# The second layer's first matmul in Strassen's seven products, in blocks of 1024 tokens

## The chip, the cores and the metric

One core of one Trainium2 chip runs the whole program. The metric is device microseconds (us) of one execution, the median of several runs.

## The reference

Chunked attention with eight memory keys per head (4 x 8 heads, 768 positions, 64 wide) gives 3072 tokens of 512. Two layers follow, each with `w_in` (512 x 2048) and `w_out` (2048 x 512):

```python
h = x @ w_in;  g = h - np.tanh(h);                              x = g @ w_out   # first layer
h = x @ w_in;  g = np.maximum(h, 0) + alpha * np.minimum(h, 0); y = g @ w_out   # second layer
```

The weights arrive as 64-bit floats. `alpha` is a vector of 2048.

## The kernel before

Tokens lie in 24 tiles of 128. Each layer takes them in six blocks of four tiles (512 columns); `d_ff` is cut into 16 slices `f` of 128. Every float is split into a high and a low part of the matmul's own 32-bit type, and a product of two floats is three passes (`PASS`: high-high, high-low, low-high). So `emit_h` (L166) issues 12 matmuls for one slice (4 depths of 128 by 3 passes) and `emit_y` (L201) issues 12 more into four PSUM banks that gather `y` over the 16 slices; the h of the next slice is issued ahead of the y of this one. Between them stands `emit_g` (L181): in the second layer two VectorE (DVE) instructions (L191, L194), then the split of g, high part on ScalarE (ACT, L197), low part on GpSimd (POOL, L198). `evac_y` (L223) copies the banks to SBUF and stores them: `y1d` in DRAM after layer one, the output after layer two.

Attention (`emit_scores`, `emit_soft`, `emit_pv`) makes the operand tiles of layer one in the double ring `ring`, four tiles ahead of time at the start and then one every 20 us or so by a plan. In one tile of it POOL multiplies the exponentials `sc` by the reciprocal of their sum (L332), DVE transposes them into `et` (L336), ACT and DVE copy `et` into `ebuf`, PE multiplies by v, and ACT and DVE split the result into `ring` (L361, L362).

Weights: `load_raw` brings 64-bit words, `to_f32` (L92) makes floats in one ACT and three DVE instructions, `split_f32` (L111) splits them on ACT and POOL. Layer one's weights are so prepared during the start and the first block. Layer two's are prepared during blocks 1 to 4 of layer one and parked in DRAM (`park`, L127), and `unpark` (L133) brings them into the pool `w` of 34 buffers of 4 KB per partition in block 5, as layer one's slices end. `load_x2` and `split_x2` bring a block of y1 back and split it.

`alpha_sb` is loaded by one DMA (L490) in the start, and used first in layer two (L191). A scheduler orders each engine's instructions when the program is built; each engine then runs its own list in order, and so does the DMA queue on SP.

## Time and profile before

| | us |
|---|---|
| three runs | 1151.85, 1153.46, 1153.91 |
| median | 1153.46 |
| the profiled execution | 1150.37 |
| its span in the profile | 1148.5 |

All that follows is read from the one profiled execution; 1.9 us of it lie outside the span. In the profile PE is the matmul engine and PEld its weight loads. A matmul's listed duration overlaps the next one's, so PE's pace is read from the distance of starts. What stands behind `<-` in brackets is what ended an engine's wait. The granted clock (PEclk) is a share of 2.4 GHz.

### The profile page before, as it was taken

How to read it: one execution, taken by the hardware profiler on the slowest of the kernel's cores; microseconds unless marked ns; L12 is line 12 of the kernel's file. 1: busy time of each engine (PE TensorE's matmuls, PEld its weight loads, DVE VectorE, ACT ScalarE, POOL GpSimd, SP SyncE). 2: the span in 40 equal slices, each digit the busy share in tenths (PEclk: the TensorE clock that was granted, in tenths of full speed). 3: DMA queues.
4: the chain of work that ended last, by engine and by line, in shares of the span. 5: the costliest groups of instructions: out<-in, count | busy, mean ns of one | idle time of the engine just before them, and what ended most of it. 6: DMA issues, size and time to landing. Idle time of an engine off the chain costs nothing.

```text
span 1148.5 us, 15553 instructions
## 1 busy us (share of the span) xinstructions
PE 1114.7 (97%) x6144; PEld 915.6 (80%) x6144; DVE 485.5 (42%) x806; ACT 345.5 (30%) x612; POOL 363.1 (32%) x299
## 2 busy tenths in 40 slices
PE   3798999999999999999999999999999999999998
PEld 3587788888888887887888888888888888888886
DVE  6998635554554544553113224234224224322322
ACT  4665534444343444443222112112112112111111
POOL 4465533433243333332221222222222222222221
PEclk9699999999999999999999999999999999999999
DMA  9772334344444444436665002002002000000000
GB/s 256 260 271 81 104 115 142 125 150 138 147 144 151 140 135 145 149 109 222 204 198 183 1 1 74 1 1 74 1 1 67 7 1 19 19 1 13 25 1 37
DMA packets 53689, 112.16 MB, mean 98 GB/s; under 512 B 7281, under 2 KB 25713, under 8 KB 53617
## 3 DMA queue, kind: packets, MB, share of 16 engines
q1 hardware_dynamic: 40944, 104.89, 28.0%
q10 hardware_dynamic: 12672, 6.29, 1.9%
q8 instruction: 48, 0.79, 0.3%
q14 instruction: 25, 0.20, 0.1%
HBM read 81.80 MB, written 29.36 MB: 97 GB/s over the span
## 4 chain that ended last, share of the span: by engine, by line
PE 88%; DMA 4%; DVE 3%; issue 2%; SPq 1%; POOL 1%; ACT 0%; DVEq 0%; POOLq 0%; ACTq 0%
PE h L173 42%; PE y L217 23%; PE y L212 20%; PE pv L354 2%; PE sp L302 1%; DMA ri<-in_moe_w_in_dram 1%; DMA alpha_sb<-in_moe_alpha_dram 1%; DVE u L102 1%; DMA y1d<-ys 1%; SPq L276 1%; DVE s L106 1%; DVE u L99 1%; DVE ebuf L345 0%; DMA vn<-in_v_dram 0%; DMA w2d<-pk 0%
## 5 line engine op out<-in xcount | busy, mean ns | idle before, releaser
L173 PE MATMUL h<-ring,wt 128*128 128x512 f32 x2304 | 561.2, 392 | 8.9 <-DVE t L189 6.0
L173 PEld LDWEIGHTS h<-ring,wt 128*128 128x128 f32 x2304 | 434.5, 189 | 103.8 <-DVE t L189 8.6
L198 POOL TENSOR_TENSOR gl<-t,gh 128x512 fp32r<-128x512 f32 x192 | 249.2, 1298 | 599.9 <-ACT gh L197 589.3
L197 ACT ACTIVATE gh<-t 128x512 fp32r<-128x512 f32 x192 | 121.2, 631 | 465.7 <-DVE t L194 407.9
L191 DVE TENSOR_SCALAR t<-h,alpha_sb 128x512 f32<-128x512 f32 x96 | 72.1, 751 | 341.6 <-PE h L173 331.8
L212 PE MATMUL y<-gh,wt 128*128 128x512 f32 x768 | 193.7, 391 | 0.0
L217 PE MATMUL y<-wt,gh 128*128 128x512 f32 x768 | 191.6, 389 | 0.0
L212 PEld LDWEIGHTS y<-gh,wt 128*128 128x128 f32 x768 | 143.2, 188 | 31.7 <-issue 2.0
L217 PEld LDWEIGHTS y<-wt,gh 128*128 128x128 f32 x768 | 144.2, 188 | 29.9
L189 DVE TENSOR_TENSOR t<-h,t 128x512 f32<-128x512 f32 x96 | 65.9, 688 | 213.2 <-ACT t L188 198.2
L188 ACT ACTIVATE t<-h 128x512 f32<-128x512 f32 x96 | 57.1, 595 | 184.9 <-PE h L173 169.2
L212 PE MATMUL y<-gl,wt 128*128 128x512 f32 x384 | 105.4, 390 | 0.0
L217 PE MATMUL y<-wt,gl 128*128 128x512 f32 x384 | 104.6, 389 | 0.0
L212 PEld LDWEIGHTS y<-gl,wt 128*128 128x128 f32 x384 | 72.0, 188 | 15.7 <-POOL gl L198 0.4
L217 PEld LDWEIGHTS y<-wt,gl 128*128 128x128 f32 x384 | 72.1, 188 | 15.0
L113 POOL TENSOR_TENSOR pk<-s,pk 128x512 fp32r<-128x512 f32 x32 | 41.6, 1301 | 105.6 <-ACT pk L112 105.6
L194 DVE SCALAR_TENSOR_TENSOR t<-h,t 128x512 f32<-128x512 f32 x96 | 66.4, 691 | 3.2
L113 POOL TENSOR_TENSOR wt<-s,wt 128x512 fp32r<-128x512 f32 x32 | 41.4, 1295 | 39.5 <-ACT wt L112 39.1
L99 DVE TENSOR_SCALAR u<-u 128x512 uint32<-128x512 uint32 x64 | 44.2, 691 | 7.6 <-ACT u L96 7.4
L343 ACT ACTIVATE ebuf<-et 32x256 f32<-32x256 f32 x96 | 39.8, 415 | 8.9 <-DVE et L336 7.4
L345 DVE COPY ebuf<-et 32x256 f32<-32x256 f32 x96 | 39.0, 407 | 1.8
L354 PEld LDWEIGHTS pv<-ebuf,vn 96*64 96x64 f32 x768 | 26.8, 148 | 15.8 <-ACT ebuf L343 7.3
(44 smaller groups left out, 476.8 us busy)
## 6 DMA issues: line engine op xcount, KB each, us to landing
w2d<-pk SPq DMA_DIRECT2D x32, 512.0 KB, 2.6
wt<-w2d SPq DMA_DIRECT2D x32, 512.0 KB, 3.8
vn<-in_v_dram SPq DMA_DIRECT2D x24, 384.0 KB, 4.2
ri<-in_moe_w_in_dram SPq DMA_DIRECT2D x16, 512.0 KB, 6.8
ro<-in_moe_w_out_dram SPq DMA_DIRECT2D x16, 512.0 KB, 7.7
pk<-in_moe_w_in_dram SPq DMA_DIRECT2D x16, 512.0 KB, 3.6
pk<-in_moe_w_out_dram SPq DMA_DIRECT2D x16, 512.0 KB, 3.5
kbuf<-in_k_dram SPq DMA_DIRECT2D x80, 96.0 KB, 3.4
```

The source lines that it names most:

```text
L99: nc.vector.tensor_scalar(out=u, in0=u, scalar1=3, scalar2=None, op0=ALU.logical_shift_left)
L113: nc.gpsimd.tensor_tensor(out=lo, in0=v, in1=f32(hi), op=ALU.subtract)
L173: last["ffn"] = nc.tensor.matmul(out=h, lhsT=wi[:, a, kk, :], rhs=ring[c][:, s0:s0 + n, kk, :], start=(i == 0), stop=(i == 3 * KD - 1),).ins
L188: nc.scalar.activation(out=t, in_=h, func=ACTF.Tanh)
L189: nc.vector.tensor_tensor(out=t, in0=h, in1=t, op=ALU.subtract)
L191: nc.vector.tensor_scalar(out=t, in0=h, scalar1=0.0, scalar2=alpha_sb[:, f:f + 1], op0=ALU.min, op1=ALU.mult)
L194: nc.vector.scalar_tensor_tensor(out=t, in0=h, scalar=0.0, in1=t, op0=ALU.max, op1=ALU.add)
L197: nc.scalar.activation(out=gh, in_=t, func=ACTF.Copy)
L198: nc.gpsimd.tensor_tensor(out=gl, in0=t, in1=f32(gh), op=ALU.subtract)
L212: mm = nc.tensor.matmul(out=yp[l, b][j][:, :n * 128], lhsT=wo[:, a, j * 128:(j + 1) * 128], rhs=g[c], start=first, stop=final,)
L217: mm = nc.tensor.matmul(out=yp[l, b][j], lhsT=g[a][:, j * 128:(j + 1) * 128], rhs=wo[:, c, :], start=first, stop=final,)
L354: last["at"] = nc.tensor.matmul(out=pv[D * j:D * j + D, 128 * p + 64 * a:128 * p + 64 * a + 64], lhsT=vt[t][:, a, D * h:D * h + D], rhs=eb ...
```

## The change

Layer two takes three blocks of 1024 tokens. In a block the two halves of tokens, of depth (512 = 2 x 256) and of a pair of slices `f` make 2 x 2 matrices, and `pair_h` forms h of the pair from seven products (1, 6, 5, 2, 7, 3, 4) of 6 matmuls each, with sums of weights and of x made beforehand. Some products add into the same PSUM bank after DVE or ACT has read it (`hs`, `hu`, `hv`). All 16 slices of g of a block stay in the pool `w` (16 buffers, `g2`); then `split_g2` splits slice after slice and `block_y` issues 24 matmuls each, into eight banks. `prelu` is two ACT instructions and one DVE instruction. The seven weight operands of a pair are computed while parking (`park_in`, `park_sum`) and streamed back, pair after pair and block after block (`load_in`: three DMAs of 512 KB and one of 256 KB); `w_out` is streamed through the free ring (`load_out`). `x2_work` loads, sums and splits the x operands of a block. `alpha_neg` is -alpha, computed on POOL. `sc` and `et` of attention move to other pools. The diff, cut to its core (lines of the new kernel are cited with its own numbers, L362 for `product`, L370 to L372 for `prelu`, L379 for `add`, L397 for `hs`):

```diff
-SCB = 2
...
+    alpha_neg = const.tile([128, NF], FP32, name="alpha_neg")
-    w2d = [dr_p.tile([128, 2 * 512], FP32, name=f"w2d{i}") for i in range(2 * NF)]
+    w2i = [dr_p.tile([128, 7 * 512], FP32, name=f"w2i{i}") for i in range(NF // 2)]
+    w2o = [dr_p.tile([128, 2 * 512], FP32, name=f"w2o{i}") for i in range(NF)]
...
+    def park_sum(p, half):
+        lo, hi = slice(0, 256), slice(256, 512)
+        v0, v1 = sw[0], sw[1]
+        s = t_p.tile([128, 512], FP32, tag="t", name="sm")
+        if half == 0:
+            nc.vector.tensor_tensor(out=s[:, hi], in0=v1[:, lo], in1=v1[:, hi], op=ALU.add)
+            nc.vector.tensor_tensor(out=s[:, lo], in0=s[:, hi], in1=v0[:, lo], op=ALU.subtract)
+            sw["s2"] = s
...
+        w = w_p.tile([128, 1024], FP32R, tag="w", name="ws")
+        split_f32(s, w[:, 0:512], w[:, 512:1024])
+        c = 1024 * (1 + half)
+        nc.sync.dma_start(out=w2i[p][:, c:c + 1024], in_=f32(w))
...
+    def load_out(i):
+        f = i % NF
+        r, c = divmod(i % 8, 4)
+        w = ring[r][:, 2 * c:2 * c + 2].rearrange("p i k c -> p (i k c)")
+        nc.sync.dma_start(out=f32(w), in_=w2o[f])
+        wo2[i] = w.rearrange("p (a n) -> p a n", a=2)
+
+    def load_in(i, q):
+        p = i % P2
+        n = 2 if q < 3 else 1
+        pool, tag = (w_p, "w") if i % 2 == 0 else (stage["z"], "z")
+        w = pool.tile([128, 2, n, 256], FP32R, tag=tag, name="wi2")
+        nc.sync.dma_start(
+            out=f32(w).rearrange("p a s n -> p (a s n)"),
+            in_=w2i[p][:, 1024 * q:1024 * q + 512 * n])
+        win[i, q] = w
...
+    def x2_work(b):
+        return ([lambda w=w: load_x2(b, w) for w in (12, 11, 22, 21)]
+                + [lambda m=m: sum_x2(b, m) for m in (5, 6, 7, 4)]
+                + [lambda m=m: split_x2(b, m) for m in ORDER])
+
+    def product(h, i, m, first):
+        b = i // P2
+        s = WSLOT[m]
+        w, x = win[i, s // 2][:, :, s % 2], xop[b, m]
+        j = 0
+        for kt in range(2):
+            for a, c in PASS:
+                nc.tensor.matmul(
+                    out=h, lhsT=w[:, a, 128 * kt:128 * kt + 128], rhs=x[c][:, kt, :],
+                    start=(first and j == 0), stop=(j == 5), skip_group_check=True,
+                )
+                j += 1
+
+    def prelu(t, h, f):
+        n = t_p.tile([128, 512], FP32, tag="t", name="n")
+        nc.scalar.activation(out=n, in_=h, func=ACTF.Relu, scale=-1.0)
+        nc.scalar.activation(out=n, in_=n, func=ACTF.Copy, scale=alpha_neg[:, f:f + 1])
+        nc.vector.scalar_tensor_tensor(
+            out=t, in0=h, scalar=0.0, in1=n, op0=ALU.max, op1=ALU.add
+        )
+
+    def pair_h(i):
...
+        product(bank(1), i, 1, True)
+        hs = g_p.tile([128, 512], FP32, tag="gh", name="hs")
+        nc.scalar.activation(out=hs, in_=d[1], func=ACTF.Copy)
+        product(bank(6), i, 6, True)
+        hu = g_p.tile([128, 512], FP32, tag="gl", name="hu")
+        add(hu, d[6], hs)
+        product(bank(5), i, 5, True)
+        hv = g_p.tile([128, 512], FP32, tag="gh", name="hv")
+        add(hv, d[5], hu)
+        product(d[1], i, 2, False)
+        prelu(ga[0], d[1], f)
+        product(bank(7), i, 7, True)
+        add(gb[1], d[7], hv)
+        prelu(gb[1], gb[1], f + 1)
+        product(d[5], i, 3, False)
+        add(ga[1], d[5], hu)
+        prelu(ga[1], ga[1], f)
+        product(d[7], i, 4, False)
+        add(gb[0], d[7], hu)
+        prelu(gb[0], gb[0], f + 1)
+
+    def split_g2(b, f):
+        hi = w_p.tile([128, 2, 512], FP32R, tag="w", name="g2h")
+        lo = w_p.tile([128, 2, 512], FP32R, tag="w", name="g2l")
+        split_f32(g2.pop((b, f)), hi, lo)
+        gsp[b, f] = (hi, lo)
+
+    def block_y(b, f):
...
+        for k in halves:
+            for n, (a, c) in enumerate(PASS):
+                for j in range(4):
+                    nc.tensor.matmul(
+                        out=sets[k][j], lhsT=g[a][:, k, j * 128:(j + 1) * 128], rhs=w[:, c, :],
+                        start=(f == 0 and n == 0), stop=(f == NF - 1 and n == 2),
+                    )
...
-        sc = aw.tile([128, H, 64], FP32, tag="sc", name="sc", bufs=SCB)
+        if t <= NS:
+            sc = w_p.tile([128, H, 64], FP32, tag="w", name="sc")
+        else:
+            sc = aw.tile([128, H, 64], FP32, tag="sc", name="sc", bufs=1)
...
-        et = aw.tile([128, H, 2, CH], FP32, tag="et", name="et", bufs=1)
+        et = t_p.tile([128, 512], FP32, tag="t", name="et")
+        et = et.rearrange("q h (s n) -> q h s n", h=H, s=2)
...
         nc.sync.dma_start(out=alpha_sb, in_=alpha.rearrange("(k p) -> p k", p=128))
+        nc.gpsimd.tensor_scalar(
+            out=alpha_neg, in0=alpha_sb, scalar1=-1.0, scalar2=None, op0=ALU.mult
+        )
...
+            if 0 < b < N1 - 1:
+                park_step((b - 1) * NF + f)
...
+                    work = x2_work(0) + [lambda q=q: load_in(0, q) for q in range(4)]
...
+                for _ in range(2):
+                    if f >= 1 and work:
+                        work.pop(0)()
...
+        NB = NTILE // 8
+        for b in range(NB):
+            more = b + 1 < NB
+            for p in range(P2):
+                i = b * P2 + p
+                if i > 0:
+                    pair_h(i)
...
+                if p + 2 < P2:
+                    for q in range(4):
+                        load_in(i + 2, q)
+            split_g2(b, 0)
+            split_g2(b, 1)
...
+            for f in range(NF):
+                if f + 2 < NF:
+                    split_g2(b, f + 2)
+                block_y(b, f)
+                if f + 8 < NF or more:
+                    load_out(b * NF + f + 8)
+                for _ in range(2):
+                    if work:
+                        work.pop(0)()
+            store_y(b)
```

Three places in the lists of instructions.

POOL, in the start (`sc` the exponentials, `sg` their reciprocal sums, `mx` their maxima, `wt` a weight being split). Before:

```order
L332 TENSOR_TENSOR sc_233<-sc_233,sg_262 128x512 [waits DVE_49]
L332 TENSOR_TENSOR sc_256<-sc_256,sg_319 128x512 [waits DVE_49,Activation_49]
L319 TENSOR_TENSOR sc_313<-sc_313,mx_314 128x512 [waits DVE_49]
L332 TENSOR_TENSOR sc_313<-sc_313,sg_375 128x512 [waits DVE_49,Activation_49]
L332 TENSOR_TENSOR sc_370<-sc_370,sg_455 128x512 [waits DVE_49,Activation_49,Pool_49]
L113 TENSOR_TENSOR wt_396<-s_394,wt_396 128x512 [waits Activation_49]
L113 TENSOR_TENSOR wt_405<-s_403,wt_405 128x512 [waits Activation_49]
```

With the change:

```order
L533 TENSOR_TENSOR sc_226<-sc_226,sg_255 128x512 [waits DVE_49,Activation_49]
L520 TENSOR_TENSOR sc_306<-sc_306,mx_307 128x512 [waits DVE_49]
L533 TENSOR_TENSOR sc_249<-sc_249,sg_312 128x512 [waits DVE_49]
L692 TENSOR_SCALAR alpha_neg_79<-alpha_sb_78 128x16 [waits DMAHW0_49]
L533 TENSOR_TENSOR sc_306<-sc_306,sg_368 128x512 [waits DVE_49,Activation_49]
L533 TENSOR_TENSOR sc_363<-sc_363,sg_448 128x512 [waits DVE_49,Activation_49]
L114 TENSOR_TENSOR wt_389<-s_387,wt_389 128x512 [waits Activation_49]
```

The negation of alpha now stands ahead of the multiplications of tiles 2 and 3 (`sc_306`, `sc_363`; before `sc_313`, `sc_370`), and waits for a DMA.

DVE, in the start (`u`, `s`: steps of `to_f32`; `et` the transposed exponentials; `pv`, `ring`: the split of attention's result). Before:

```order
L362 TENSOR_TENSOR ring1_113<-pv_277,ring0_112 128x512 [waits Activation_49]
L336 STREAM_TRANSPOSE et_380<-sc_313 128x512 [waits Pool_49]
L102 SCALAR_TENSOR_TENSOR u_390<-ri_183,u_390 128x512 [waits DMAHW0_49,DVE_49]
L331 RECIPROCAL sg_455<-sg_455 128x8 [waits DVE_49]
L99 TENSOR_SCALAR u_399<-u_399 128x512 [waits Activation_49]
L345 COPY ebuf_125<-et_380 32x8x32 [waits DVE_49,PE_49]
L345 COPY ebuf_125<-et_380 32x8x32 x3
L362 TENSOR_TENSOR ring1_113<-pv_334,ring0_112 128x512 [waits Activation_49]
```

With the change:

```order
L103 SCALAR_TENSOR_TENSOR u_383<-ri_176,u_383 128x512 [waits DMAHW0_49,DVE_49]
L532 RECIPROCAL sg_368<-sg_368 128x8 [waits DVE_49]
L103 SCALAR_TENSOR_TENSOR u_392<-ro_178,u_392 128x512 [waits DMAHW1_49,DVE_49]
L532 RECIPROCAL sg_448<-sg_448 128x8 [waits DVE_49]
L564 TENSOR_TENSOR ring1_106<-pv_270,ring0_105 128x512 [waits Activation_49]
L538 STREAM_TRANSPOSE et_373<-sc_306 128x512 [waits Pool_49]
L107 SCALAR_TENSOR_TENSOR s_387<-ri_176,u_383 128x512 [waits DVE_49]
L107 SCALAR_TENSOR_TENSOR s_396<-ro_178,u_392 128x512 [waits DVE_49]
```

The transposition of tile 2 (`et_380` before, `et_373` now) still stands in the midst of the weight work; the second weight's first steps (`u_392`) are now ahead of it.

DVE in layer two, a steady stretch (`h` PSUM of `emit_h`; `h2` banks of the products; `g2` the kept g; `n` of `prelu`). Before, two instructions a slice:

```order
L191 TENSOR_SCALAR t_7302<-h_7289,alpha_sb_78 128x512 [waits DMAHW7_49,PE_49,Activation_49]
L194 SCALAR_TENSOR_TENSOR t_7302<-h_7289,t_7302 128x512 [waits DVE_49]
L191 TENSOR_SCALAR t_7338<-h_7325,alpha_sb_78 128x512 [waits DMAHW0_49,PE_49]
L194 SCALAR_TENSOR_TENSOR t_7338<-h_7325,t_7338 128x512 [waits DVE_49]
L191 TENSOR_SCALAR t_7370<-h_7357,alpha_sb_78 128x512 [waits DMAHW1_49,PE_49,Activation_49]
L194 SCALAR_TENSOR_TENSOR t_7370<-h_7357,t_7370 128x512 [waits DVE_49]
```

With the change, nine a pair (`hu_6097`, `hv_6106` belong to the next pair):

```order
L372 SCALAR_TENSOR_TENSOR g2_5998<-h2_6000,n_6033 128x512 [waits Activation_49]
L379 TENSOR_TENSOR g2_5999<-h2_6037,hv_6025 128x512 [waits DMAHW2_49,DVE_49,PE_49]
L379 TENSOR_TENSOR g2_5998<-h2_6018,hu_6016 128x512 [waits PE_49]
L372 SCALAR_TENSOR_TENSOR g2_5999<-g2_5999,n_6045 128x512 [waits DVE_49,Activation_49]
L379 TENSOR_TENSOR hu_6097<-h2_6090,hs_6088 128x512 [waits Activation_49]
L372 SCALAR_TENSOR_TENSOR g2_5998<-g2_5998,n_6056 128x512 [waits DVE_49,Activation_49]
L379 TENSOR_TENSOR g2_5999<-h2_6037,hu_6016 128x512 [waits PE_49]
L379 TENSOR_TENSOR hv_6106<-h2_6099,hu_6097 128x512 [waits DVE_49,PE_49]
L372 SCALAR_TENSOR_TENSOR g2_5999<-g2_5999,n_6067 128x512 [waits DVE_49,Activation_49]
L372 SCALAR_TENSOR_TENSOR g2_6079<-h2_6081,n_6114 128x512 [waits DMAHW1_49,Activation_49]
```

The additions of one pair now alternate with ACT's work on the same pair, and the first sums of the next pair are in between. On PE the products of neighbouring pairs are interleaved there, in the order 7, 6', 3, 1', 4, 5', 2' (the dash marks the next pair).

## Rows read from the trace of the kernel before

**Rows 1.** The page, busy time of each engine.

```profile
PE 1114.7 (97%) x6144; PEld 915.6 (80%) x6144; DVE 485.5 (42%) x806; ACT 345.5 (30%) x612; POOL 363.1 (32%) x299
```

**Rows 2.** Stretches: length, busy time (count) per engine, granted clock, DMA share, GB/s.

```profile
28.70:57.40 28.70, 21.73 (x176) 16.93 (x177) 26.64 (x50) 17.38 (x34) 14.20 (x12) 0.70 0.74 260
57.40:86.00 28.60, 28.52 (x153) 23.02 (x152) 27.08 (x48) 18.89 (x36) 19.94 (x16) 1.00 0.74 271
200.00:300.00 100.00, 100.00 (x658) 82.09 (x657) 51.11 (x93) 43.02 (x79) 35.92 (x29) 1.00 0.44 142
530.00:621.00 91.00, 90.49 (x400) 74.62 (x399) 16.66 (x26) 24.63 (x42) 23.73 (x18) 1.00 0.63 208
621.00:1143.50 522.50, 522.50 (x2306) 432.46 (x2304) 159.92 (x221) 76.43 (x126) 124.84 (x96) 1.00 0.06 21
```

**Rows 3.** Timeline of PE in layer two: start, length, instructions.

```profile
632.00 2.88 PE L173 MATMUL h<-ring,wt 128*128 128x512 f32 x12
634.72 1.98 PE L217 MATMUL y<-wt,gh 128*128 128x512 f32 x8
```

**Rows 4.** Timeline of PE in the start.

```profile
38.92 0.80 PE L173 MATMUL h<-ring,wt 128*128 128x512 f32 x1 [1.90 <-ACT ring L361]
40.60 8.11 PE L173 MATMUL h<-ring,wt 128*128 128x512 f32 x23 [0.89 <-DVE ring L362]
50.65 3.01 PE L173 MATMUL h<-ring,wt 128*128 128x512 f32 x12 [1.94 <-DVE t L189]
```

**Rows 5.** The tile alpha_sb: its users, its DMA's issue, time to landing.

```profile
L191 DVE TENSOR_SCALAR t<-h,alpha_sb x96: 741/752/753, 621.4 to 1138.2; 128x512 f32<-128x512 f32 x96
L490 SPq DMA_DIRECT2D alpha_sb<-in_moe_alpha_dram x1: 379/379/379, 29.5 to 29.5; - x1
...
DMA to landing us min/median/max: 9.8/9.8/9.8
```

**Rows 6.** Timeline of POOL in the start.

```profile
24.92 1.04 POOL L332 TENSOR_TENSOR sc<-sc,sg 128x512 f32<-128x512 f32 x1 [3.61 <-DVE sg L331]
28.07 1.04 POOL L332 TENSOR_TENSOR sc<-sc,sg 128x512 f32<-128x512 f32 x1 [2.11 <-DVE sg L331]
```

**Rows 7.** Timeline of DVE in the start.

```profile
26.51 0.70 DVE L336 STREAM_TRANSPOSE et<-sc 128x512 f32<-128x512 f32 x1
...
49.91 0.68 DVE L189 TENSOR_TENSOR t<-h,t 128x512 f32<-128x512 f32 x1
```

**Rows 8.** Groups of instructions: count, busy us, mean ns.

```profile
L173 PE MATMUL h<-ring,wt 128*128 128x512 f32 x2304 | 561.2, 392 | 8.9 <-DVE t L189 6.0 <-ACT ring L361 1.9 <-DVE ring L362 0.9
L198 POOL TENSOR_TENSOR gl<-t,gh 128x512 fp32r<-128x512 f32 x192 | 249.2, 1298 | 599.9 <-ACT gh L197 589.3 <-PE y L212 4.3 <-DMA pk<-in_moe_w_in_dram 3.2
L197 ACT ACTIVATE gh<-t 128x512 fp32r<-128x512 f32 x192 | 121.2, 631 | 465.7 <-DVE t L194 407.9 <-DVE t L189 37.4 <-PE y L217 10.9
L194 DVE SCALAR_TENSOR_TENSOR t<-h,t 128x512 f32<-128x512 f32 x96 | 66.4, 691 | 3.2
L251 DVE TENSOR_TENSOR ring<-x,ring 128x512 fp32r<-128x512 f32 x24 | 19.6, 868 | 0.0
```

**Rows 9.** The line L251 alone: shortest, median, longest in ns.

```profile
L251 DVE TENSOR_TENSOR ring<-x,ring x24: 682/686/1779, 529.4 to 967.2; 128x512 fp32r<-128x512 f32 x24
```

**Rows 10.** Timeline of the last slices and the end.

```profile
1138.20 0.75 DVE L191 TENSOR_SCALAR t<-h,alpha_sb 128x512 f32<-128x512 f32 x1 [3.96 <-PE h L173]
1138.98 0.69 DVE L194 SCALAR_TENSOR_TENSOR t<-h,t 128x512 f32<-128x512 f32 x1
1139.79 0.63 ACT L197 ACTIVATE gh<-t 128x512 fp32r<-128x512 f32 x1 [4.81 <-DVE t L194]
1142.46 1.07 PE L217 MATMUL y<-wt,gl 128*128 128x512 f32 x4
1143.51 1.80 SPq L237 DMA_DIRECT2D out_dram<-ys  x4
```

**Rows 11.** DMA issues: count, KB each, median us to landing.

```profile
wt<-w2d SPq DMA_DIRECT2D x32, 512.0 KB, 3.8
out_dram<-ys SPq DMA_DIRECT2D x24, 256.0 KB, 2.5
```

More of the change, by code (lines that the diff above doesn't have):

```diff
@@ L125, in split_w, with park_in @@
         keep(l, f, got)
-    def park(i):
-        raw = raws.pop((1, i))
+    sw = {}
+    def park_in(f):
+        raw = raws.pop((1, 2 * f))
+        v = aw.tile([128, 512], FP32, tag="v", name="wv")
+        v = to_f32(raw, v)
+        w = raw.bitcast(FP32R)
+        p, odd = divmod(f, 2)
+        sw[odd] = v
+        if odd:
+            split_f32(v[:, 256:512], w[:, 0:256], w[:, 256:512])
+            nc.sync.dma_start(out=w2i[p][:, 3072:3584], in_=f32(w)[:, 0:512])
+        else:
+            split_f32(v, w[:, 0:512], w[:, 512:1024])
+            nc.sync.dma_start(out=w2i[p][:, 0:1024], in_=f32(w))
@@ L129, in park, with park_out @@
+    def park_out(f):
+        raw = raws.pop((1, 2 * f + 1))
         w = raw.bitcast(FP32R)
         split_f32(to_f32(raw), w[:, 0:512], w[:, 512:1024])
-        nc.sync.dma_start(out=w2d[i], in_=f32(w))
-    def unpark(f):
-        got = []
-        for side in range(2):
-            w = w_p.tile([128, 2, 512], FP32R, tag="w", name="wt")
-            nc.sync.dma_start(out=f32(w).rearrange("p a n -> p (a n)"), in_=w2d[2 * f + side])
-            got.append(w)
-        keep(1, f, got)
+        nc.sync.dma_start(out=w2o[f], in_=f32(w))
@@ new lines, in load_x2, with sum_x2 @@
+    def load_x2(b, which):
+        k, t = which // 10 - 1, which % 10 - 1
+        r = w_p.tile([128, 2, 512], FP32R, tag="w", name="x2")
+        nc.sync.dma_start(out=f32(r), in_=y1d[2 * b + t, :, 2 * k:2 * k + 2, :])
+        xin[b, which] = r
+    def sum_x2(b, m):
+        p, q = {5: (12, 11), 6: (22, 5), 7: (22, 12), 4: (21, 6)}[m]
+        t = w_p.tile([128, 2, 512], FP32, tag="w", name="xt")
+        nc.vector.tensor_tensor(
+            out=t, in0=f32(xin[b, p]), in1=f32(xin[b, q]), op=ALU.subtract
+        )
+        xin[b, m] = t
@@ new lines, in pair_h, with bank @@
+    def pair_h(i):
+        b, p = divmod(i, P2)
+        f = 2 * p
+        add = lambda o, p, q: nc.vector.tensor_tensor(out=o, in0=p, in1=q, op=ALU.add)
+        d = {}
+        for j in range(2):
+            g2[b, f + j] = w_p.tile([128, 2, 512], FP32, tag="w", name="g2")
+        ga, gb = [[g2[b, f + j][:, k] for k in range(2)] for j in range(2)]
+        def bank(m):
+            if b > 0:
+                t = ps_y.tile([128, 512], FP32, tag="y", name="h2")
+            elif m in (1, 5):
+                t = ps_h.tile([128, 512], FP32, tag="h", name="h2")
+            else:
+                t = ps_h2.tile([128, 512], FP32, tag="h2", name="h2")
+            d[m] = t
+            return t
+        product(bank(1), i, 1, True)
[18 more added lines that the diff above has]
+        prelu(gb[0], gb[0], f + 1)
@@ new lines, in split_g2 @@
+    def split_g2(b, f):
[4 more added lines that the diff above has]
+    def block_y(b, f):
+        if f == 0:
+            sets = [[ps_y.tile([128, 512], FP32, tag="y", name="y") for _ in range(4)], [
+                pool.tile([128, 512], FP32, tag=tag, name="yb")
+                for pool, tag in ((ps_h, "h"), (ps_h2, "h2")) for _ in range(2)]]
+            yp[1, b] = sets
+        sets = yp[1, b]
+        g = gsp.pop((b, f))
+        w = wo2.pop(b * NF + f)
+        halves = (1, 0) if f == 0 and b > 0 else (0, 1)
+        for k in halves:
[4 more added lines that the diff above has]
+                        start=(f == 0 and n == 0), stop=(f == NF - 1 and n == 2),
+                    )
```

143 lines of the change are left out of this document (100 added, 43 removed).

## The prediction

> **What bounds the kernel now.** I read the shares of the page first: PE is busy in 97% of the span, DVE in 42%, ACT and POOL in about 30% [rows 1]. Busy PE could still be slow PE, so I went to the stretches next: in all of layer two, from 621.0 to 1143.5, PE is busy in 522.5 of 522.5 us at full granted clock [rows 2]. The pace is read from starts: twelve matmuls of h begin at 632.00, the y behind them at 634.72 [rows 3], so one matmul takes 2.72 / 12 = 0.2267 us, and 522.5 / 2306 gives the same. In the middle of layer one PE is busy in all of 100 us too, with DVE at half. Only the start is different: from 28.7 to 57.4 PE has 21.7 of 28.7 us, the clock is 0.70, and DVE has 26.6, so there DVE bounds; from 57.4 on PE has 28.5 of 28.6 us with DVE still at 27.1 [rows 2]. Two things follow. A matmul taken from layer two is worth its 0.2267 us as long as its operands come in time; and a DVE stall in the start moves everything behind it, since PE never idles enough later to make it up.
>
> **The change, part by part.** All is summed against the profiled execution of 1150.4 us.
>
> *Matmuls.* h of layer two was 6 blocks x 16 slices x 12 = 1152 matmuls. Now it is 3 blocks x 8 pairs x 7 products x 6 = 1008. y stays at 1152 (6 x 16 x 12; 3 x 16 x 24). So 144 x 0.2267 = **-32.6 us**. All are again 128x512 with a 128-wide weight load, so I keep the pace.
>
> *The wait for alpha.* alpha's DMA is issued at 29.5 and lands 9.8 us later, at 39.3; before, nobody used it until 621.4 [rows 5]. SP's list ahead of it is unchanged. Now POOL negates alpha, and this stands ahead of the multiplications of tiles 2 and 3, which ran at 24.9 and 28.1 [rows 6]. POOL is stuck from before 24.9 to 39.3; tile 2's multiplication ends at 39.4 + 1.04 = 40.4. DVE's transposition of that tile, at 26.5 before [rows 7], waits for it, and behind it in DVE's list stand all the rest of the start, weights too. So DVE is put back by 40.4 - 26.5 = 13.9 us, less what the new order does ahead of the transposition: three 0.69 us steps of a weight, 2.0 us. That is 11.9. Following the list row by row to the first h and its subtraction (at 49.9 before, and the third h at 50.65 behind it [rows 4, 7]), I come to 12 to 13.4, as some waits of DVE for ACT open again. I take **+12.5**. The ends: 0, if the place in the list did not hold anyone up; 15, if ACT's queue, stuck behind the same tile, adds a microsecond. No gain is possible, since nothing becomes earlier. DVE runs at 9 tenths until 86 us, so I let it make up nothing.
>
> *The elementwise work of h.* A pair has nine DVE instructions (0.69 us, L194) and nine of ACT (0.63, L197) [rows 8]: 6.2 and 5.7 us beside 42 x 0.2267 = 9.5 us of PE. That is enough room in sum, but they alternate, in fixed order. I laid out one pair with PE's seven products of 1.36 us each, 0.16 us for a matmul's last result (0.39 listed [rows 8] against 0.227) and 0.12 us from engine to engine (DVE ends 1139.67, ACT starts 1139.79 [rows 10]). With product 7 at zero, product 3 ends at 4.08. Then DVE adds ga1 (4.35 to 5.05) and finishes gb1 (to 5.75); ACT takes relu of ga1 (5.15 to 5.8), then hs' of the next pair (to 6.4); DVE adds hu' (6.5 to 7.2); ACT scales (6.4 to 7.05); DVE finishes ga1 (7.2 to 7.9) and adds gb0 (to 8.6). Only then is the bank free that product 7' needs at 9.52. The slack is 0.8 us, the least of all; the other banks are ready 1.7 us or more ahead. So **0**, covered by PE's own products; if the cover goes, each microsecond is paid 24 times. No gain is possible here.
>
> *The end of layer one.* In four slices of block 5 POOL gets two x splits of 1024 columns each beside gl. A 1024-wide one lies between 1.30 us (the 512-wide row [rows 8]) and twice that; I take 2.6, as for work that goes column by column. A slice then wants 2 x 2.6 + 1.3 = 6.5 us of POOL against 5.44 of PE: 4 x 1.1 = 4.2 us too much, from which the lists' lookahead (an h ahead, over 2 us) is taken off. I take **+1**, from 0 to 4.2.
>
> Here a rule bears on DVE's four sums of x, which read two SBUF tiles while POOL reads SBUF. The row: L251, of the same kind, has a median of 686 ns and once 1779 [rows 9]; its 24 take 19.6 us, 3.1 more than 24 medians [rows 8], 0.13 each, so 0.5 us for four. The Trainium skill (SBUF — State Buffer, Who interferes with whom) says that a DVE instruction with two SBUF inputs and a GpSimd instruction that reads SBUF block each other for a whole instruction. By it all four sums meet a split, some 5 us more; by the row mostly none do.
>
> *The joints.* From h to y the first g is split (ACT and POOL, up to 3.9 us) while the last pair still has two products of PE, and the list mixes y in. Later in y POOL has 16 splits of g and 7 of x in a block, 23 x 2.6 = 60 us beside 16 x 5.44 = 87 of PE: covered. From y to h four banks are emptied while PE works 2.7 us on the other four. I take **+1** for the five joints, from 0 to 5.
>
> *Streams.* A pair's weights are 7 x 256 KB = 1.84 MB in 9.5 us, 193 GB/s. The stretch of unparking moved 208 at a DMA share of 0.63 [rows 2], and a load of 512 KB lands in 3.8 us [rows 11] when the next use is over 10 us off. On SP each waits for a tile that PE has left, nearly a pair earlier. Cost 0.
>
> *Layer one.* Parking gets two sums and two more splits a pair, and `sc` and `et` share buffers. PE has 100 of 100 us there with POOL at 36 and DVE at 51 [rows 2]: hidden, 0. Without that cover a late gl would hold y.
>
> *The tail.* The last matmul ends at 1143.5, the stores issue until 1145.3 [rows 10]. Now the last four copies wait for buffers of the first four (2.5 us to land [rows 11]): **+1**, from 0 to 2.
>
> Sum: -32.6 + 12.5 + 1 + 1 + 1 = -17.1, so 1133.3 for a profiled execution. The median of the runs shown is 3.1 us above that of the profile; I keep that distance: **1136**.
>
> **The rivals.**
> *Alpha's wait is hidden.* Speaks for it: POOL is lightly used and its list catches up within a few instructions. Against: DVE, not POOL, bounds the start, and it stands behind POOL. Time: 1136 - 12.5 = 1124.
> *Sums and splits block each other* at the end of layer one, each of the four by 1.1 us (1.78 - 0.69): 1136 + 4 = 1140. One such row in 24 speaks for it, the median against. This is what the page of the Trainium skill named above would make of it.
> *Slower: product 7' waits in every pair.* The place is DVE's list between ga1 and gb0. Two of its steps there read SBUF twice. At 1.78 us each [rows 9] the chain is 2.2 longer, 1.4 over the slack, 24 times: 1136 + 34 = 1170. It costs from 0.8 us on, and makes the kernel slower than before from 1.6. Against it: POOL, which may be what stretched that row, is idle in this stage.
> *The weights do not stream as the change says they should.* Below 193 GB/s PE waits for them; at the 142 GB/s that layer one moved [rows 2] a pair takes 12.9 us, and 24 x 3.4 us bring 1218. Against it: 271 GB/s in the start.
>
> **How the numbers follow.** A measurement of this kernel can tell about 0.2%, 2.3 us. Forecast 0.67, hidden alpha 0.10, blocking sums 0.08, chain 0.09, streams 0.03, and 0.03 for stalls I do not see. The forecast's own terms reach from 1132 to 1147. The range from 1122 to 1150 adds the hidden alpha and the blocking sums and leaves out the two slow cases. Faster: 0.67 + 0.10 + 0.08 = 0.85; within 0.2%: 0.03, from the unseen stalls; slower 0.12.
>
> **What would show it.** Right: 6000 PE matmuls; POOL idle from about 22 to 39 us, ended by alpha's DMA; the third h at 62 to 64 us; layer two at 0.2267 us a matmul, 490 us long, with PE idle under 2 us in it. Wrong: the third h before 55 us (alpha hidden); PE waiting for DVE ahead of each seventh product (the chain), or for a DMA of `w2i` (streams); PE idle above 5 us around the end of layer one.

## The result, and the profile after the change

The changed kernel takes **1131.73 us** (median of 4 runs, 1131.53 to 1133.19) against 1152.65 us for the kernel before (4 runs): ratio 0.9825, 95% interval 0.9803 to 0.9846, so 1.5 to 2.0% faster. The forecast was 1136, with a range of 1122 to 1150. The profiled execution of the changed kernel took 1133.19 us (span 1131.4) where the sum had 1133.3. That agreement is partly luck: four terms were off, and the errors cancelled.

The page's first lines, to set beside [rows 1]:

```profile
span 1131.4 us, 15773 instructions
PE 1083.9 (96%) x6000; PEld 888.3 (79%) x6000; DVE 532.7 (47%) x850; ACT 481.0 (43%) x793; POOL 431.9 (38%) x289
```

6000 matmuls, 144 fewer, and PE is still the engine that bounds. The stretches, to set beside [rows 2]: length, busy time (count) of PE, PEld, DVE, ACT and POOL, granted clock, DMA share, GB/s.

```profile
28.70:57.40 28.70, 10.09 (x126) 8.24 (x123) 16.85 (x37) 11.68 (x24) 8.38 (x8) 0.87 0.60 217
200.00:300.00 100.00, 100.00 (x655) 81.80 (x654) 53.26 (x98) 44.18 (x81) 42.70 (x35) 1.00 0.49 165
550.00:600.00 50.00, 50.00 (x222) 41.43 (x221) 13.10 (x15) 18.94 (x27) 30.10 (x17) 1.00 0.29 98
641.00:1131.40 490.40, 483.54 (x2132) 399.83 (x2131) 185.63 (x236) 202.30 (x291) 158.35 (x62) 1.00 0.44 146
```

The loss is in the first of them: PE has 10.1 of 28.7 us there instead of 21.7, and DVE, which bounded that stretch, 16.9 instead of 26.6. Why DVE stood still is read from POOL's timeline and then DVE's (start, duration, instruction, in brackets the idle time before it and what ended it):

```profile
20.40 1.04 POOL L533 TENSOR_TENSOR sc<-sc,sg 128x512 f32<-128x512 f32 x1
39.84 0.26 POOL L692 TENSOR_SCALAR alpha_neg<-alpha_sb 128x16 f32<-128x16 f32 x1 [18.40 <-DMA alpha_sb<-in_moe_alpha_dram]
40.05 2.04 POOL L533 TENSOR_TENSOR sc<-sc,sg 128x512 f32<-128x512 f32 x2
```
```profile
41.13 0.71 DVE L538 STREAM_TRANSPOSE et<-sc 128x512 f32<-128x512 f32 x1 [10.81 <-POOL sc L533]
...
64.37 0.68 DVE L255 TENSOR_TENSOR t<-h,t 128x512 f32<-128x512 f32 x1
```

POOL stands 18.4 us for alpha, then come the multiplications of tiles 2 and 3, and DVE's transposition of tile 2 is at 41.1 instead of 26.5 [rows 7]. PE's third h follows at 65.64 instead of 50.65 [rows 4]:

```profile
52.96 0.80 PE L239 MATMUL h<-ring,wt 128*128 128x512 f32 x1 [0.70 <-ACT ring L563]
55.16 7.79 PE L239 MATMUL h<-ring,wt 128*128 128x512 f32 x23 [1.41 <-DVE ring L564]
64.56 1.15 PE L556 MATMUL pv<-ebuf,vn 96*64 96x64 f32 x32 [1.61 <-issue]
65.64 3.01 PE L239 MATMUL h<-ring,wt 128*128 128x512 f32 x12
```

In all of layer two PE has one idle time that the list of waits names, near its beginning; then PE's last group:

```profile
655.46 0.50 PE L362 MATMUL h<-xh,wi 128*128 128x512 f32 x1 [1.78 <-DVE g L372]
...
1125.26 1.07 PE L435 MATMUL yb<-ring,g2l 128*128 128x512 f32 x4
```

These lines give a balance of the two profiled spans. Layer two is now 2160 matmuls, 489.6 us at the 0.2267 us that also hold here, plus the gap of 1.8; counted back from the end of PE's last group (1126.3) it begins at 634.9. Before, 2304 matmuls (522.3 us) ended at 1143.5 [rows 10], so it began at 621.2. The first row of the table is thus a count times the pace, and the second is what is left over: the sum closes by construction. That a matmul really costs its pace is tested below by an eighth product, and the start by other runs.

| part | forecast | measured |
| --- | --- | --- |
| 144 matmuls fewer | -32.6 | -32.7 |
| everything up to layer two | +12.5 and +1 | +13.7 |
| gaps of PE in layer two (forecast: five joints) | +1 | +1.8 |
| from the last matmul to the end | +1 | +0.1 (5.1 after 5.0) |
| sum | -17.1 | -17.1 (1148.5 to 1131.4) |

### The profile page after: what moved, and what is told of

It reads as the page before. It is cut to its first block, busy times and chain, and to the rows that moved or that the text cites. A ratio compares the mean times of both kernels' runs of the same rounds, so it can differ in the third digit from the quotient of the medians.

```text
span 1131.4 us, 15773 instructions
## 1 busy us (share of the span) xinstructions
PE 1083.9 (96%) x6000; PEld 888.3 (79%) x6000; DVE 532.7 (47%) x850; ACT 481.0 (43%) x793; POOL 431.9 (38%) x289
## 4 chain that ended last, share of the span: by engine, by line
PE 64%; DMA 2%; issue 1%; ACT 1%; DVE 1%; POOL 0%; SPq 0%; POOLq 0%; DVEq 0%; ACTq 0%
PE h L362 19%; PE y L435 11%; PE yb L435 11%; PE y L278 10%; PE h L239 10%; DMA pk<-in_moe_w_in_dram 1%; DMA y1d<-ys 1%; PE pv L556 1%; PE sp L500 1%; DMA w2o<-pk 0%; DMA out_dram<-ys 0%; ACT n L370 0%; ACT n L371 0%; DVE g L372 0%; DVE t L255 0%
## 5 line engine op out<-in xcount | busy, mean ns | idle before, releaser
L239 PE MATMUL h<-ring,wt 128*128 128x512 f32 x1152 | 282.5, 394 | 4.7 <-DVE t L255 2.6
L239 PEld LDWEIGHTS h<-ring,wt 128*128 128x128 f32 x1152 | 216.7, 189 | 54.3 <-DVE t L255 5.0
L114 POOL TENSOR_TENSOR g2l<-g,g2h 128x1024 fp32r<-128x1024 f32 x48 | 121.7, 2570 | 283.4 <-ACT g2h L113 283.4
L362 PE MATMUL h<-xh,wi 128*128 128x512 f32 x672 | 208.7, 389 | 1.8 <-DVE g L372 1.8
L264 POOL TENSOR_TENSOR gl<-t,gh 128x512 fp32r<-128x512 f32 x96 | 126.7, 1322 | 151.8 <-ACT gh L263 123.7
L362 PEld LDWEIGHTS h<-xh,wi 128*128 128x128 f32 x672 | 126.2, 188 | 28.2 <-DVE g L372 2.2
L435 PE MATMUL y<-ring,g2h 128*128 128x512 f32 x384 | 95.8, 389 | 0.0
L435 PE MATMUL yb<-ring,g2h 128*128 128x512 f32 x384 | 95.6, 389 | 0.0
L435 PEld LDWEIGHTS yb<-ring,g2h 128*128 128x128 f32 x384 | 72.1, 188 | 14.9
L370 ACT ACTIVATE n<-g 128x512 f32<-128x512 f32 x72 | 45.3, 632 | 72.7 <-DVE g L379 72.6
L362 PE MATMUL h<-xl,wi 128*128 128x512 f32 x192 | 74.7, 389 | 0.0
L372 DVE SCALAR_TENSOR_TENSOR g<-g,n 128x512 f32<-128x512 f32 x72 | 62.6, 869 | 17.0 <-ACT n L371 15.7
```

Source lines behind the costliest of these rows:

```text
L114: nc.gpsimd.tensor_tensor(out=lo, in0=v, in1=f32(hi), op=ALU.subtract)
L239: last["ffn"] = nc.tensor.matmul(out=h, lhsT=wi[:, a, kk, :], rhs=ring[c][:, s0:s0 + n, kk, :], start=(i == 0), stop=(i == 3 * KD - 1),).ins
L264: nc.gpsimd.tensor_tensor(out=gl, in0=t, in1=f32(gh), op=ALU.subtract)
L362: nc.tensor.matmul(out=h, lhsT=w[:, a, 128 * kt:128 * kt + 128], rhs=x[c][:, kt, :], start=(first and j == 0), stop=(j == 5), skip_group_c ...
L370: nc.scalar.activation(out=n, in_=h, func=ACTF.Relu, scale=-1.0)
L372: nc.vector.scalar_tensor_tensor(out=t, in0=h, scalar=0.0, in1=n, op0=ALU.max, op1=ALU.add)
```

## The experiments

Twelve kernels were run. The kernel before was timed again beside each set, with medians from 1151.5 to 1152.6. Each edit is one to the changed kernel unless said otherwise.

### What the start costs, and why

**alpha loaded first, or negated late.** Two ways to take POOL's wait away.

```diff
         nc.vector.memset(ebuf, 0.0)
+        nc.sync.dma_start(out=alpha_sb, in_=alpha.rearrange("(k p) -> p k", p=128))
...
-        nc.sync.dma_start(out=alpha_sb, in_=alpha.rearrange("(k p) -> p k", p=128))
         nc.gpsimd.tensor_scalar(
```

> Only alpha's load is moved: from SP's place after the first weights to the very first load of the program, so that the negation on POOL never waits; the lists of PE, DVE and ACT stay as in the changed kernel. Theory A (POOL's wait for alpha is the whole loss of the start, 13.7 us at the end of layer one): the third h starts at 50 to 53 us instead of 65.6, and the median is 1118 us (1116 to 1120). Rival B (the new order of the weight steps costs part of it): third h at 55 to 62, 1121 to 1129. Rival C (the wait was hidden and something else delays the start): 1131 to 1133.

Measured: 1124.5 us (four runs in two pairs: 1122.2 and 1122.9, 1126.1 and 1126.6). In the second run the negation's result moved to a small pool that opens when attention's closes, so that POOL does it at 527 us.

> alpha's load stays where the changed kernel has it; the negation moves to POOL's list of block 5, behind all of attention. Theory A: POOL has nothing to wait for at 21 us, third h at 50 to 53, median 1118 (1116 to 1120), within 1 us of the run with the early load. If instead the load itself disturbed the start, this one keeps the loss: 1128 to 1133. Rival B as in the run with the early load: 1121 to 1129.

Measured: 1128.1 us (1126.7 to 1129.0). The wait is gone in both, and neither reached 1118; the third h came at 55.10 and 54.52, not at 50 to 53. POOL's, DVE's and PE's timelines of the run with the early load, and a stretch of it:

```profile
29.37 2.04 POOL L533 TENSOR_TENSOR sc<-sc,sg 128x512 f32<-128x512 f32 x2 [8.73 <-DVE sg L532]
```
```profile
30.45 0.71 DVE L538 STREAM_TRANSPOSE et<-sc 128x512 f32<-128x512 f32 x1
```
```profile
55.10 4.43 PE L239 MATMUL h<-ring,wt 128*128 128x512 f32 x12
```
```profile
55.10:59.50 4.40, 4.40 (x15) 3.55 (x14) 4.23 (x7) 3.06 (x6) 4.40 (x4) 0.65 0.83 215
```

So alpha's wait is worth 10.5 us at the third h, and some 4 us have another cause (rival B). POOL's line points to it: even without alpha it stands 8.7 us, until DVE has done the reciprocal `sg` of tile 2, so that tile's multiplication cannot begin before 29.4, where it began at 24.9 before [rows 6]. Of POOL's 18.4 us, then, only what goes beyond this is alpha's. Of the 10.5 the end of the program keeps 6.6 in the profiled executions: the third h itself takes 4.43 us for its twelve matmuls instead of 3.01, at a granted clock of 0.65 (1.00 in the changed kernel from 65.6 to 68.7); 1.0 us is a wait of y for a copy (`ys`, L295) that the changed kernel did not have; and from 640 to 700 us there are 250 matmuls instead of 257 (1.6 us, see the last section).

**The same negation in the kernel before**, right behind alpha's load, in the same words.

```diff
         nc.sync.dma_start(out=alpha_sb, in_=alpha.rearrange("(k p) -> p k", p=128))
+        nc.gpsimd.tensor_scalar(
+            out=alpha_neg, in0=alpha_sb, scalar1=-1.0, scalar2=None, op0=ALU.mult
+        )
```

> The kernel before, with the same negation added (its result is not used). Its place in POOL's list comes out three rows later than in the changed kernel: behind the two weight splits that ran at 32.2 and 35.7 us, ahead of the multiplication that ran at 40.1. alpha lands at 39.3. Theory A (place decides, not the operation or the wait as such): POOL waits about 2 us that were idle anyway, and the time stays 1152.6 within 0.2%. Rival (a wait for alpha on POOL costs some 12 us wherever it stands in the start): 1163 to 1167.

Measured: 1152.3 us, ratio 1.0003 (0.9992 to 1.0013). POOL's timeline:

```profile
37.63 1.27 POOL L114 TENSOR_TENSOR wt<-s,wt 128x512 fp32r<-128x512 f32 x1 [2.24 <-ACT wt L113]
41.04 0.26 POOL L492 TENSOR_SCALAR alpha_neg<-alpha_sb 128x16 f32<-128x16 f32 x1 [2.14 <-DMA alpha_sb<-in_moe_alpha_dram]
42.05 1.04 POOL L333 TENSOR_TENSOR sc<-sc,sg 128x512 f32<-128x512 f32 x1 [0.75 <-DVE sg L332]
```

The wait is 2.1 us, and the multiplication behind it still waits 0.75 us for DVE: nobody was late. The operation and its wait cost nothing in this place; the place costs.

**The buffers of attention's tiles.** The change had also taken `sc` and `et` out of their own buffers. These two runs are edits to the run with alpha first. First only `et` was freed from the four that it shares with the weights' `s` and layer one's `t`:

```diff
-        et = t_p.tile([128, 512], FP32, tag="t", name="et")
+        pool, tag = (w_p, "w") if t <= NS else (t_p, "t")
+        et = pool.tile([128, 512], FP32, tag=tag, name="et")
```

> As the run with alpha's load first, and in the start the transposed tile et comes from the large pool, not from the four buffers that it shares since the change with the weights' s and layer one's t; with it DVE's list has the reciprocal of tile 2 ahead of the weight steps again, as before the change. There the third h came at 55.1 with the wait for alpha gone, against 50.65 before. Theory E (the shared buffers, and the order that they led to, are these 4.4 us): third h at 50 to 52 us, median 1120 (1117 to 1122). Rival (those 4.4 us come from elsewhere): third h at 55, 1123 to 1126.

Measured: 1123.6 us (1122.2 to 1125.7); the third h at 56.1, with y of slice 0 now ahead of it. So theory E fell in this form. Then both tiles got what they had before the change, two buffers and one, from space that only the parking needs later (the run also takes the copies of y1 out of a shared buffer, see the joint below):

```diff
-            sc = w_p.tile([128, H, 64], FP32, tag="w", name="sc")
+            sc = aw.tile([128, H, 64], FP32, tag="v", name="sc")
...
-        et = t_p.tile([128, 512], FP32, tag="t", name="et")
+        et = (aw.tile([128, 512], FP32, tag="sc", name="et", bufs=1) if t <= NS
+              else t_p.tile([128, 512], FP32, tag="t", name="et"))
```

> alpha's load first; attention's tiles sc and et in the start have two and one buffers apart from the others, as before the change (they use those that the parking of weights needs only later); the four copies of y of layer one's last block have four buffers apart from n's. DVE's list of the start is then row for row that of the kernel before, down to the third h. Theory G (the loss of the start is alpha's wait plus the order that the moved buffers led to, and nothing else): third h at 50 to 51.5 us as before the change, layer one ends within 1 us of it (equivalent of 621.2), PE's gap at 650 under 0.5 us, and the time is 621.2 + 489.6 + 5.1 + 1.9 = 1118 (1116.5 to 1120). Rival (something else of the change slows the start, such as the other order of loads on SP): third h at 53 or later, 1121 to 1124.

Measured: **1121.1 us** (1120.5 to 1122.5), ratio to the kernel before 0.9738 (0.9724 to 0.9751): the fastest of all. The third h came at 53.08, later than expected, and where its rival had put it (53 or later, 1121 to 1124). But the whole start is later in that execution, as it is in that of the kernel before with the negation, where nothing was changed ahead of it. (In this run alpha's load stands ahead of everything on SP; so it does in the run with alpha first, where `kbuf` is loaded at 17.06.) The first load of `kbuf` on SP, in the kernel before, in the kernel before with the negation, and in this run:

```profile
16.43 2.39 SPq L276 DMA_DIRECT2D kbuf<-in_k_dram  x4
```
```profile
18.44 2.39 SPq L277 DMA_DIRECT2D kbuf<-in_k_dram  x4
```
```profile
18.52 2.39 SPq L475 DMA_DIRECT2D kbuf<-in_k_dram  x4
```

Counted from that load, the executions fall into line (us):

| kernel | `kbuf` load | transposition of tile 2 | after the load | third h | after the load |
| --- | --- | --- | --- | --- | --- |
| before | 16.43 | 26.51 | 10.1 | 50.65 | 34.2 |
| before, with negation | 18.44 | 28.42 | 10.0 | 52.56 | 34.1 |
| changed | 17.32 | 41.13 | 23.8 | 65.64 | 48.3 |
| alpha first | 17.06 | 30.45 | 13.4 | 55.10 | 38.0 |
| alpha first, `et` apart | 17.07 | 29.44 | 12.4 | 56.1 | 39.0 |
| alpha first, `sc` and `et` as before | 18.52 | 28.96 | 10.4 | 53.08 | 34.6 |

Of the 14.1 us that the third h lost, 10.3 are alpha's wait and 3.4 the order that came with the moved buffers; 0.4 are left. Each is the difference of two single executions, and holds to about 1 us: six other executions whose start is that of the changed kernel (the runs of the next two parts) have the third h 47.0 to 48.2 after the load where this table has 48.3, and the late negation has it at 37.7 where alpha first has 38.0. The 0.4 are within that.

Theory G holds for the third h, by this count and not by the absolute times that it gave. It does not hold for the time. By the medians 30.4 of the 32.6 us are gained, and counted back from the end of PE's last group (1114.5) layer two begins at 624.9 instead of 621.2: 2.1 of the 3.7 are the later load, and 1.6 the third h's twelve matmuls, which take 4.61 us at a granted clock of 0.64 (3.01 at 1.00 before). Why the load and the clock differ is open.

### The joint from layer one to layer two

**Stores of y1 on SP.** ACT stands 3.5 us until a store of y1 has landed, and PE's gap of 1.8 follows:

```profile
653.33 0.60 ACT L370 ACTIVATE n<-h 128x512 f32<-128x512 f32 x1 [3.47 <-DMA y1d<-ys]
```

> The four stores of y of layer one's last block are issued by SP instead of ACT. In the changed kernel ACT stands 3.5 us behind such a store at 649.8 to 653.3, and PE then has its longest idle time in layer two, 1.8 us at 653.7. Theory D (ACT's wait at its store makes that gap): the gap goes, 1131.7 - 1.8 = 1130 us. Rival (the buffers of the copies, not ACT's place in line, make it): the gap stays at 1.8, 1131.7.

Measured: 1136.0 us (1132.5 to 1137.0), and a gap of 2.4. Of the 4.3 us that it is slower the trace shows 2.3 in the gap and the matmuls behind it (247 from 640 to 700 us instead of 257, see the last section) and 1.0 at the third h, which takes 4.01 us instead of 3.01. ACT waits for the store although SP now issues it:

```profile
655.18 0.60 ACT L370 ACTIVATE n<-h 128x512 f32<-128x512 f32 x1 [4.14 <-DMA y1d<-ys]
```

Theory D fell: what ACT waits for is the buffer. The tiles `n` of the first pair and the four copies `ys` share four.

**Buffers apart for the copies.** Three of 2 KB fitted; the pool `stage["ys"]` opens when attention's closes.

```diff
-            s = t_p.tile([128, 512], FP32, tag="t", name="ys")
+            s = (stage["ys"].tile([128, 512], FP32, tag="ys", name="ys") if b == N1 - 1
+                 else t_p.tile([128, 512], FP32, tag="t", name="ys"))
```

> The changed kernel, but the four copies of y of layer one's last block have three buffers of their own instead of the four that they share with the tiles n of layer two's first pair; stores stay on ACT. Moving only the stores to SP had left the gap (2.4 us). Theory F (n waits for a buffer whose store is under way): PE's idle time of 1.8 us at 653 falls under 0.5 us, and the median to 1128 to 1130.5. Rival (the copies themselves, not their buffers, are late): the gap stays, 1131 to 1133.

Measured: 1133.8 us (1132.3 to 1136.4), no gain, and a gap of 1.6. It is the rival's number with another wait behind it: the fourth copy now stands for the store of the first.

```profile
645.23 0.69 DVE L298 COPY ys<-y 128x512 f32<-128x512 f32 x1 [4.01 <-DMA y1d<-ys]
```

**All three mends, with three buffers for the copies.** These are alpha first, `et` apart and the copies apart.

> All three mends together: alpha's load first, et in the start from the large pool, buffers of their own for the copies of layer one's last block. If they add up: 1131.7 - 7.2 (alpha first, measured) - 4.4 - 1.8 = 1118 (1115 to 1121), layer two without a wait of PE above 0.5 us. If DVE in the start takes back a part, as it did with alpha first (10.5 us at the third h, 7.2 in the time): 1120 to 1124.

Measured: 1122.7 us (1121.7 to 1124.0), a gap of 1.1; the mends do not add up. The fastest run, above, took the fourth copy from the shared four and three from their own. There PE's waits from 58 us to the end are these two lines, and none is in layer two:

```profile
PE h L239 <- DVE t L255: 2.3, 4, 0.7
PE y L278 <- ACT ys L296: 0.6, 1, 0.6
```

So theory F holds with four buffers, for the gap. What a gap of 1.8 us is worth is read from traces alone, 1.8 us or 3.4 (see the last section); the two runs that changed only this place were no faster than the changed kernel.

### The stage of the seven products

**An eighth product.** The first product of each pair is computed twice.

```diff
         product(bank(1), i, 1, True)
+        product(d[1], i, 1, True)
```

> The first product of each pair is computed twice (the second overwrites the first), so h of layer two takes 1152 matmuls again, as many as the kernel before. Theory (PE alone sets the pace of this stage, 0.2267 us a matmul): 1131.7 + 144 x 0.2267 = 1164 us (1162 to 1167). Rival (the elementwise chain or the streams set part of the pace, so that extra PE work fits into waits): below 1155.

Measured: 1168.0 us (1164.0 to 1168.8), 36.3 more by the medians. The profiled one of these runs took 1164.0, 30.8 more than the profiled run of the changed kernel, with the third h 2.4 us earlier: 33.2 for layer two, where 32.6 were expected. PE takes the whole price of a matmul. The other three runs took 1167.7 to 1168.8 and have no profile, so where their 4 us more are stays open.

**Two more DVE instructions a pair**, between the third product and the addition that frees the bank of the next seventh.

```diff
         prelu(ga[1], ga[1], f)
+        nc.vector.scalar_tensor_tensor(
+            out=hu, in0=hu, scalar=1.0, in1=hu, op0=ALU.mult, op1=ALU.max
+        )
+        nc.vector.scalar_tensor_tensor(
+            out=hu, in0=hu, scalar=1.0, in1=hu, op0=ALU.mult, op1=ALU.max
+        )
```

> Two more DVE instructions a pair, on the tile hu, ahead of the addition that frees the bank of the next seventh product; at 0.61 us from start to start, 1.2 us. In the trace of the changed kernel that bank is free 1.75 us before PE wants it (addition ends 851.0, product starts 852.9). Theory (slack 1.75 as the trace has it): no change, 1130 to 1134. Rival (slack 0.8, as the prediction laid the chain out): (1.2 - 0.8) x 24 = 10 us more, 1139 to 1144.

Measured: 1133.9 us (1131.8 to 1134.0), and no wait of PE from 660 to 1000 us. The median is 2.2 above the changed kernel's, the profiled execution 1.4 below it with the third h 1.4 earlier; no difference is shown. The slack is larger than the prediction had it. One turn in the changed kernel's DVE, in the second of layer two's three blocks, and then two lines of a turn in the first:

```profile
847.56 0.69 DVE L379 TENSOR_TENSOR g<-h,hu 128x512 f32<-128x512 f32 x1 [1.59 <-PE h L362]
848.17 0.68 DVE L372 SCALAR_TENSOR_TENSOR g<-g,n 128x512 f32<-128x512 f32 x1
848.92 0.69 DVE L379 TENSOR_TENSOR hu<-h,hs 128x512 f32<-128x512 f32 x1
849.71 0.69 DVE L372 SCALAR_TENSOR_TENSOR g<-g,n 128x512 f32<-128x512 f32 x1
850.32 0.69 DVE L379 TENSOR_TENSOR g<-h,hu 128x512 f32<-128x512 f32 x1
```
```profile
667.31 0.69 DVE L379 TENSOR_TENSOR hu<-h,hs 128x512 f32<-128x512 f32 x1 [0.70 <-ACT hs L397]
...
668.53 0.68 DVE L379 TENSOR_TENSOR g<-h,hu 128x512 f32<-128x512 f32 x1
```

The addition of ga1, the last step of gb1, hu', the last step of ga1, the addition of gb0: the bank is free at 851.0, and the seventh product starts at 852.8. The slack is 1.8 us, not 0.8. In the first block it is 1.35: the bank is free at 669.2 and the product starts at 670.56. Part of what the prediction missed is that DVE's starts lie 0.60 apart in a row. The rest, in the second and third block, is PE's order: there the products run 7, 1', 3, 6', 4, 2', 5' instead of 7, 6', 3, 1', 4, 5', 2' (the apostrophe marks the next pair), so ACT has copied hs' before ga1 is added, and DVE does not wait for it.

**POOL busy beside the products**: three subtractions of 128x1024 a pair that read SBUF, then in another run seven fills of the same size that only write.

```diff
         prelu(ga[0], d[1], f)
+        junk = stage["junk"]
+        nc.gpsimd.tensor_copy(out=junk[:, 0, 0:16], in_=ga[0][:, 0:16])
+        for _ in range(3):
+            nc.gpsimd.tensor_tensor(out=junk, in0=junk, in1=f32(xop[b, 5][1]), op=ALU.subtract)
```

> In h of layer two POOL, idle there, gets three subtractions of 128x1024 a pair that read two SBUF tiles (result not used), released by the first g of the pair. Theory (a DVE instruction that reads two SBUF tiles stands while such a POOL instruction runs; g<-g,n took 2.9 us instead of 0.69 beside POOL's splits at the end of a block): the two of them in the chain get 1 to 2.2 us longer, 2 to 4.4 in all against 1.75 of slack, so 0.3 to 2.6 us in each of 24 pairs: 1138 to 1195, PE waits for DVE ahead of seventh products, and the additions that read PSUM stay at 0.69. Rival (POOL does not matter): 1130 to 1134, g<-g,n at 0.69 throughout.

Measured: 1150.8 us (1147.2 to 1152.8), 19 more: nearly all of the change's gain is gone. DVE's and POOL's timelines:

```profile
827.95 1.32 DVE L372 SCALAR_TENSOR_TENSOR g<-g,n 128x512 f32<-128x512 f32 x1 [0.86 <-ACT n L371]
829.19 0.68 DVE L379 TENSOR_TENSOR hu<-h,hs 128x512 f32<-128x512 f32 x1
829.79 2.28 DVE L372 SCALAR_TENSOR_TENSOR g<-g,n 128x512 f32<-128x512 f32 x1
832.00 0.68 DVE L379 TENSOR_TENSOR g<-h,hu 128x512 f32<-128x512 f32 x1
```
```profile
826.30 8.04 POOL L409 TENSOR_TENSOR junk<-junk,xl 128x1024 f32<-128x1024 f32 x3
```

The two steps that read two SBUF tiles take 1.32 and 2.28 us, together 2.2 more than the 0.69 each of before; the additions that read PSUM stay at 0.68. The chain is over its slack of 1.8, and a pair takes 9.87 us (832.00 to the next such addition at 841.87) instead of 9.52.

That alone would be 24 x 0.35 = 8 us, not 19. The profiled executions (1147.3 and 1131.4) show where the rest is. With the third h 2.2 earlier, layer two is 18.1 us longer: 3.6 in the pairs of each of the second and third block, 7.2 in those of the first, and 3.7 at the joints from h to y and back. Of the 7.2, 5.0 lie ahead of the first block's third pair, where the gap at the joint from layer one has grown from 1.8 us:

```profile
656.36 0.79 PE L362 MATMUL h<-xh,wi 128*128 128x512 f32 x1 [4.47 <-DVE g L372]
```

> The same place and about the same time of POOL, but with seven fills of 128x1024 a pair, which write SBUF and read nothing. Theory (it is POOL's reading that blocks): g<-g,n stays at 0.69, 1130 to 1134. Rival (any POOL instruction on SBUF blocks): as in the run with the subtractions, 1138 and more.

Measured: 1133.3 us (1131.3 to 1135.8). The same step beside the fills (min/median/max in ns; the maximum is beside the splits at a block's end), and the fills:

```profile
L372 DVE SCALAR_TENSOR_TENSOR g<-g,n x72: 681/690/2893, 645.4 to 1045.4; 128x512 f32<-128x512 f32 x72
```
```profile
L409 POOL MEMSET junk<- 128x1024 f32 x168 | 160.7, 956 | 8.8
```

It is POOL's reading that stretches such a DVE instruction, not POOL's being busy.

## Why the prediction came out right

*Matmuls, -32.6.* Right: an eighth product in each pair, 144 matmuls more, costs 33.2 us in the profiled execution.

*The wait for alpha, +12.5.* Right in the mechanism, near in size by luck, wrong in its parts. The step that failed is the credit, "less what the new order does ahead of the transposition: three 0.69 us steps of a weight, 2.0 us". The new order was a loss: steps of a weight now stand ahead of the reciprocal, so with the wait gone POOL multiplies at 29.4 instead of 24.9, and the transposition comes 3.3 us later (13.4 against 10.1 after `kbuf`'s load). From the transposition to the subtraction of the first h, behind which the third h follows, DVE needs 23.2 us (41.13 to 64.37) where it needed 23.4 [rows 7], so nothing was won there either. The wait itself was taken too large, at 13.9 for 10.7 (41.13 less the 30.45 of the run without it). The two errors have opposite signs. Behind them stands "`sc` and `et` share buffers ... hidden, 0": hidden in the middle of layer one, where PE has 100 of 100 us, but the start, where DVE bounds, was not costed. The third h came at 65.6, beyond the 62 to 64 that were to show this step right (in the six other executions with this start at 63.3 to 65.4).

*The end of layer one, +1.* It cost nothing that the trace shows. The sums run at 557 to 565 us and the splits to 588, and PE is busy in 50 of 50 us from 550 to 600, with 222 matmuls, as many as before; no wait of PE lies between the start and layer two but 2.6 us for `t`, less than the 4.1 that the kernel before had there.

*Sums and splits that block each other.* The blocking came, where the prediction held that mostly it would not; the price did not. At the end of layer one two of the four sums took 1.2 us and two 1.7 and 1.9, and inside layer two, beside the splits of g, they looked like this:

```profile
719.98 2.75 DVE L338 TENSOR_TENSOR xt<-x,x 128x1024 f32<-128x1024 f32 x1 [0.61 <-DMA x<-y1d]
722.65 2.88 DVE L372 SCALAR_TENSOR_TENSOR g<-g,n 128x512 f32<-128x512 f32 x1
725.45 3.41 DVE L338 TENSOR_TENSOR xt<-x,xt 128x1024 f32<-128x1024 f32 x1
```
```profile
711.22 19.91 POOL L114 TENSOR_TENSOR g2l<-g,g2h 128x1024 fp32r<-128x1024 f32 x7 [77.14 <-ACT g2h L113]
```

All of that stands beside y, which runs 384 matmuls, 87 us, and needs of it only the splits of the last slices' g. By the rule of the Trainium skill (SBUF — State Buffer, Who interferes with whom), a DVE instruction with two SBUF inputs contends with a GpSimd instruction that reads SBUF and not with one that only writes; the three runs and these lines agree with both halves.

*The elementwise chain, 0, and the rival of 1170.* Right that it is covered. The slack was mis-sized: 0.8 was worked out from listed durations of 0.69 and one order of the products, but DVE's starts lie 0.60 apart in a row, and two of the three blocks run another order; the bank was free 1.35 us ahead in the first block and 1.8 in the others. The rival's mechanism is real: POOL's reads beside the products brought 1150.8. The argument against it, that POOL is idle in this stage, was the right one.

*Joints, +1.* The five joints between h and y cost nothing that the list of waits names; the 1.8 are at a joint that was not counted, from layer one to layer two, over four buffers that layer one's last copies share with `n`.

*Streams, 0.* Right: no wait of PE for a DMA in layer two.

*The tail, +1.* It cost 0.1.

*From the sum to the median, +3.1.* Wrong: the median lies 1.5 us below the changed kernel's profiled run. The profiled run of the kernel before had an early start (`kbuf`'s load at 16.43; 18.44 with the same list on SP in another), so its distance to the median was a matter of that execution and should not have been carried over. These 3.1 are the larger part of the 4.3 us between 1136 and 1131.7; the rest is that the changed kernel's profiled run was the slowest of its four.

## What to carry to other kernels

A tiny operation that waits for a late transfer costs what stands behind it in its engine's list: find the place where the scheduler put it, and who waits there, before pricing it. An edit that takes a tile out of its buffers is an edit of the order: cost it in every stage that uses the tile, above all in the one where that engine bounds. Before comparing starts of two executions, count from the same load; and do not carry one execution's distance to a median over to another kernel.
